# A retention layer and two gated layers on one core: loads, q scaling and the state sum of the first sequence set in another order

## The chip, the cores and the metric

The kernel runs on one core of a Trainium2 chip. The metric is the device time of one execution in microseconds; the median of three runs of the kernel before is 584.75 us (584.52 to 586.34). TensorE (PE) multiplies matrices, with its weight loads as a row of their own (PEld), VectorE (DVE), ScalarE (ACT) and GpSimd (POOL) do the elementwise work, and SyncE (SP) issues all DMAs.

## The reference

Three layers in a row: a linear attention with a decaying state, and two layers of the form "expand to 2048, nonlinearity, contract to 512" on 1536 tokens. The weights come as 64-bit floats.

```
state = gamma * state + k[t] (outer) v[t]      # 2 sequences, 8 heads, 768 steps, head size 64
y[t]  = q[t] @ state / sqrt(64)
h = y @ w_in;  g = max(h, 0) + alpha * min(h, 0);  x = g @ w_out
h = x @ w2_in; g = (a0 + a1 h + a2 h^2 + a3 h^3) / (1 + |b0||h| + |b1| h^2 + 1e-6);  out = g @ w2_out
```

## The kernel before

The attention is done in chunks of 128 steps, six to a sequence, chunks 0 to 5 and 6 to 11. For a chunk c, `att_b(c)` makes the scores: eight matmuls `sc` of k (transposed) and q, which VectorE multiplies by a table of decays (`dm_sb`) into `s`; and it scales q, in place, by a column of constants on ScalarE and by a table (`dq_sb`) on GpSimd for c < 4, else on VectorE. `att_k(c)` scales k (on GpSimd, or on ScalarE for 4 <= c < 8). `att_c(c)` makes the output in a PSUM bank `y`: eight matmuls of v and `s`, then the state product (`st`, eight matmuls of k and v in a bank of their own for the first sequence), then eight matmuls of the state `R` and the scaled q, summed into `y`. The state product is then added to `R` (copied to it for a first chunk), and `y` is split in two rounded parts, `xh` (ScalarE) and `xl` (VectorE, the remainder), so that a product of two such pairs takes three matmuls.

Each of the 64 weight tiles (512 KB as 64-bit words, `r`) is turned into a pair of that kind by `w_abs` (ScalarE), `w_word` in three parts (VectorE: a shift, L284, and two joins, L288 and L292; the tile is `z`), `w_hi` (ScalarE, `wh`) and `w_lo` (VectorE, `wl`). The tables `START` and `dec` (lines 245 to 250 and 482 to 486) say in which half step each of the four is done.

The two gated layers are 96 steps of `pe_h` (twelve matmuls into a bank `h`), a nonlinearity (`act1_*`, `act2_*`) whose result is again split into a pair, and `pe_out` (twelve matmuls into four accumulator banks, `acc`). Chunks 4 to 11 of the attention run between the first steps; `stages` says where. The order of each engine's queue is the order of the code: `tc.manual_schedule()` moves nothing. So an operation that waits holds up whatever stands behind it on its engine.

PSUM has eight banks: a ring of four (`rbank`; scores, `h`, and for chunks from 4 on `y` and `st` too) and the four accumulators (`abank`, which chunks 0 to 3 use for `y` and `st`). SBUF tiles come from a list of 42 slots that are used in turn (`alloc`, `drop`). DMAs all go through SyncE's queue, in code order, eight in flight: the ninth is issued when the first has landed. `keep_warm` puts matmuls of zeros between the first chunks.

The stretch at the start is written out in a list:

```
order = [("b", 0), ("c", 0), ("b", 1), ("b", 2), ("c", 1), ("b", 3), ("c", 2), ("c", 3)]
```

after which the loop over steps begins with h0 (step 0), chunk 4's `att_c`, chunk 5's `att_b`, h1, chunk 5's `att_c`, chunk 6's `att_b`, h2, and `pe_out(0)`.

Of the kernel before, what the change touches and what calls it, by code (L numbers as in the profile page):

```python
# [14 lines left out]
P = 128  # L15
# [3 lines left out]
NK = 4  # L19
# [12 lines left out]
def tile_fused(  # L32
# [71 lines left out]

    def load_nv(c):
        nc.sync.dma_start(out=att[c]["k"], in_=kn[c])
        nc.sync.dma_start(out=att[c]["v"], in_=vn[c])

# [17 lines left out]
    def rows(c, j):  # L126
# [3 lines left out]
        return [(h[1], h[0]), (h[0], h[1])]  # L130

    def att_b(c, bank):
        a = att[c]
        ps = [bank(f"sc{c}_{e}") for e in range(2)]
        for j in range(NK):
            js = slice(j * P, (j + 1) * P)
            for e in range(2):
                es = slice(64 * e, 64 * e + 64)
                nc.tensor.matmul(ps[e][:, js], a["t"][es, js], a["q"][es, js], start=True, stop=True)  # L139
        a["s"] = alloc(f"s{c}")  # L140
        for e in range(2):
            es = slice(512 * e, 512 * e + 512)
            nc.vector.tensor_tensor(out=a["s"][:, es], in0=ps[e], in1=dm_sb[:, es], op=ALU.mult)  # L143
        if c % CPB > 0:
            a["qs"] = a["t"] if c > CPB else a["q"]
            for j in range(NK):
                js = slice(j * P, (j + 1) * P)
                o = 8 * CPB + 4 * (c % CPB) + j
                for ds, es in rows(c, j):
                    nc.scalar.mul(a["qs"][ds, js], a["q"][es, js], cst_sb[es, o:o + 1])  # L150
            eng = nc.gpsimd if c < 4 else nc.vector
            eng.tensor_tensor(out=a["qs"], in0=a["qs"], in1=dq_sb, op=ALU.mult)

    def att_c(c, ybank, pbank):
# [13 lines left out]
        for j, e in heads:  # L168
# [7 lines left out]
            )  # L176
        if not last:
            pst = ys[0][:, 256:512] if four else pbank(f"st{c}")[:, 0:256]
            for j, g in heads:
# [7 lines left out]
                    stop=not four or (first and j == NK - 1),  # L187
                )
        if not first:
            for j, e in heads:  # L190
# [8 lines left out]
                )  # L199
        if not last:  # L200
            src = pst.rearrange("p (j d) -> p j d", j=NK)
            if first:
                nc.scalar.copy(R, src)
            else:
                nc.vector.tensor_tensor(out=R, in0=R, in1=src, op=ALU.add)
        b, o = divmod(c * P, TB)
        osl = slice(o, o + P)
        for n, y in enumerate(ys):
# [6 lines left out]
            )  # L215
        for nm in ("qk", "kv", "s"):
            drop(a[nm])

# [27 lines left out]
    for m in A:  # L246
        START[0, m, 0], START[0, m, 1] = 2 * m - 9, 2 * m - 4
    START[0, 0, 0] = -10
    for j, m in enumerate(B):
# [76 lines left out]
    def pe_h(i):  # L326
        l, b, m, _, _ = STEPS[i]
        wh, wl = W[l, m, 0]
        ps = ring.tile([P, 512], F32, tag="ring", name=f"h{i}")
        n = 0  # L330
        for k in range(NK):
            ks = slice(k * P, (k + 1) * P)
            for w, hl in ((wh, 0), (wh, 1), (wl, 0)):
                nc.tensor.matmul(ps, w[:, ks], xs(hl, b, k, ALL), start=(n == 0), stop=(n == 11))  # L334
                n += 1
        H[i] = ps
# [91 lines left out]
    def act2_split(i):  # L428
        gh, gl = G[i]
        a, t = T3.pop(i)  # L430
        nc.scalar.copy(gh, a)  # L431
        eng = nc.gpsimd if i < NSTEP - 2 else nc.vector
        eng.tensor_tensor(out=gl, in0=a, in1=gh.bitcast(F32), op=ALU.subtract)  # L433
        drop(t)
# [49 lines left out]
    for k, e in enumerate(SEQ):  # L484
        for o, nm in zip((0, 1, 2, 3) if k != 1 else (0, 2, 3, 3), ("abs", "word", "hi", "lo")):
            dec.setdefault(START[e] + o, []).append((nm, k))
# [3 lines left out]
    def half(t, scalar_last=None, between=None):  # L490
# [21 lines left out]
        if later and t % 2 == 0:  # L512
            split_x(*later.pop(0))
        load_next(3 if t < -6 else 4 if t < 2 * N1 else 2)

    with tc.manual_schedule():
# [6 lines left out]
        nc.scalar.preload_act_table_set("natural_log_exp_and_others")  # L523
        for c in range(4):
            att_tiles(c)
# [3 lines left out]
        load_nv(0)  # L529
        load_kq(1)  # L530
        load_next(1)
        load_kq(2)
        load_nv(1)
        nc.sync.dma_start(out=dq_sb, in_=dq)
        load_kq(3)
        load_nv(2)
        load_nv(3)
        load_next(3)
        nc.sync.dma_start(out=alpha_sb, in_=alpha)
        nc.sync.dma_start(out=ab_sb[:, 0:4], in_=pa.partition_broadcast(P))  # L540
# [9 lines left out]
        for n, (s, c) in enumerate(order):  # L550
            if n in (1, 2, 3):
                keep_warm((3, 2, 3)[n - 1])
            if s == "b":
                att_k(c)
                att_b(c, rbank)
            else:
                att_c(c, abank(c % 2), abank(2 + c % 2))
                if c < 2:
                    att_load(4 + c)
            if n == 6:  # L560
                nc.scalar.activation(bb_sb[:, 0:2], ab_sb[:, 4:6], AF.Abs)
                nc.scalar.mul(nalpha_sb, alpha_sb, -1.0)
            half(n - NPRE)
        drop(wt)
        att_b(4, rbank)
# [8 lines left out]
        def stage(t):  # L574
# [12 lines left out]
            else:  # L587
                att_c(c, rbank, rbank)
                if c + 2 < NCH:
# [109 lines left out]
```

## Time and profile before

| | |
|---|---|
| runs, median (range) | 584.75 us (584.52 to 586.34) |
| profiled execution | 586.74 us |
| its span, first to last instruction | 585.0 us |
| mean granted TensorE clock | 0.997 |
| TensorE busy | 574.4 us, 98% of the span |
| VectorE, ScalarE, GpSimd busy | 468.5, 370.8, 75.4 us |
| DMA traffic | 50.78 MB; 341 GB/s on average over the first 60 us |

The profiled execution is one execution, with its own time; the views below are all of it. A timeline row gives the start from the beginning of the span, the duration, engine, line, operation, what it writes and reads, how many were merged, and in brackets how long the engine had been idle and what ended that. TensorE does a float32 matmul in two passes, so eight of them show as x16; a group is as long as the distance to the next group's start, and its last matmul's end is modelled. The granted clock is a share of 2.4 GHz: 0.50 is 1.2 GHz.

### The profile page before, as it was taken

The page shows a single profiled execution, that of the slowest core. Times are in us where ns is not written, and L with a number is a line of the kernel's source. Part 1 is how long each engine was busy: PE and PEld are TensorE (multiplying, and loading weights), DVE is VectorE, ACT ScalarE, POOL GpSimd, SP SyncE. Part 2 cuts the span into 40 slices and gives each one's busy share as a digit, 9 for nine tenths or more (in the row PEclk, how much of TensorE's full clock was granted, in tenths as well). Part 3 has the DMA queues.
Part 4 walks back from the last instruction along what each step waited for, and adds up shares of the span by engine and source line. Part 5 has one row for each costly group of instructions (what it writes and reads, how often), then busy time and mean ns, then how long its engine had stood idle before and what let it go on. Part 6 is the DMA issues. An engine that isn't in the chain of part 4 may idle for free.

```text
span 585.0 us, 8123 instructions
## 1 busy us (share of the span) xinstructions
PE 574.4 (98%) x3040; PEld 473.3 (81%) x3040; DVE 468.5 (80%) x739; ACT 370.8 (63%) x679; POOL 75.4 (13%) x60
## 2 busy tenths in 40 slices
PE   7989999999999999999999999999999999999996
PEld 7868777888888888888888888888888888888885
DVE  1899778778684364448998999999998999887886
ACT  2586667666553353436765787777786786686672
POOL 1402000000000000000000313213222221221220
PEclk8999999999999999999999999999999999999999
DMA  8999422334321012112551010001111100010101
GB/s 315 358 379 347 144 74 73 109 108 145 108 73 36 1 36 73 36 37 72 182 213 37 1 37 29 20 25 37 36 38 36 38 0 1 1 72 2 64 9 73
DMA packets 18920, 50.78 MB, mean 87 GB/s; under 512 B 2624, under 2 KB 2752, under 8 KB 18880
## 3 DMA queue, kind: packets, MB, share of 16 engines
q1 hardware_dynamic: 18880, 50.26, 24.4%
q8 instruction: 24, 0.39, 0.3%
q14 instruction: 16, 0.13, 0.1%
HBM read 47.10 MB, written 3.15 MB: 86 GB/s over the span
## 4 chain that ended last, share of the span: by engine, by line
PE 91%; DVE 5%; ACT 2%; DMA 1%; issue 1%; SPq 0%; ACTq 0%
PE acc L351 43%; PE h L334 43%; PE sc L139 1%; PE y L170 1%; DMA kv<-in_vn_dram 1%; PE y L193 1%; ACT qk L150 1%; DVE z L288 1%; DVE z L292 1%; DVE wl L309 0%; DVE p L448 0%; DVE s L143 0%; PE y L182 0%; ACT kv L120 0%; ACT g L431 0%
## 5 line engine op out<-in xcount | busy, mean ns | idle before, releaser
L334 PE MATMUL h<-xh,wh 128*128 128x512 f32 x384 | 150.3, 391 | 1.5 <-DVE xl L213 1.5
L334 PE MATMUL h<-xl,wh 128*128 128x512 f32 x384 | 149.6, 389 | 0.0
L334 PE MATMUL h<-xh,wl 128*128 128x512 f32 x384 | 149.5, 389 | 0.0
L351 PE MATMUL acc<-wh,g 128*128 128x512 f32 x384 | 126.0, 390 | 0.4 <-ACT g L431 0.4
L433 POOL TENSOR_TENSOR g<-as,g 128x512 fp32r<-128x512 f32 x46 | 62.9, 1367 | 449.5 <-PE acc L351 266.3
L351 PE MATMUL acc<-g,wh 128*128 128x512 f32 x384 | 118.9, 391 | 0.0
L334 PEld LDWEIGHTS h<-xh,wh 128*128 128x128 f32 x384 | 72.1, 188 | 17.1 <-DVE xl L213 1.7
L351 PEld LDWEIGHTS acc<-wh,g 128*128 128x128 f32 x384 | 72.0, 188 | 16.1 <-ACT g L431 0.9
L334 PEld LDWEIGHTS h<-xh,wl 128*128 128x128 f32 x384 | 72.1, 188 | 15.2
L334 PEld LDWEIGHTS h<-xl,wh 128*128 128x128 f32 x384 | 72.1, 188 | 15.0 <-DVE xl L213 0.2
L351 PEld LDWEIGHTS acc<-g,wh 128*128 128x128 f32 x384 | 71.6, 188 | 15.5 <-issue 0.7
L303 ACT CAST wh<-z 128x512 fp32r<-128x512 f32 x64 | 39.6, 619 | 57.2 <-DVE z L292 57.2
L351 PE MATMUL acc<-g,wl 128*128 128x512 f32 x192 | 74.9, 390 | 0.1
L351 PE MATMUL acc<-wl,g 128*128 128x512 f32 x192 | 74.7, 389 | 0.0
L375 DVE SCALAR_TENSOR_TENSOR np<-np,nalpha_sb 128x512 f32<-128x512 f32 x48 | 35.9, 748 | 40.5 <-ACT np L370 40.4
L369 ACT ACTIVATE np<-h 128x512 f32<-128x512 f32 x48 | 28.5, 594 | 44.3 <-PE h L334 44.2
L396 ACT ACTIVATE as<-h 128x512 f32<-128x512 f32 x48 | 28.6, 596 | 41.1 <-PE h L334 41.1
L292 DVE SCALAR_TENSOR_TENSOR z<-r,z 128x512 uint32<-128x512 uint32 x64 | 46.9, 733 | 1.5
L402 DVE SCALAR_TENSOR_TENSOR as<-as,bb_sb,rr 128x512 f32<-128x512 f32 x48 | 36.9, 768 | 13.2 <-ACT rr L397 13.2
L385 DVE TENSOR_TENSOR g<-np,g 128x512 fp32r<-128x512 f32 x48 | 33.1, 689 | 17.6 <-ACT g L380 17.3
L288 DVE SCALAR_TENSOR_TENSOR z<-r,z 128x512 uint32<-128x512 uint32 x64 | 45.6, 712 | 1.0
L309 DVE TENSOR_TENSOR wl<-z,wh 128x512 fp32r<-128x512 f32 x64 | 45.9, 717 | 0.1
(59 smaller groups left out, 751.1 us busy)
## 6 DMA issues: line engine op xcount, KB each, us to landing
r<-in_w1i_dram SPq DMA_DIRECT2D x16, 512.0 KB, 5.8
r<-in_w1o_dram SPq DMA_DIRECT2D x16, 512.0 KB, 4.3
r<-in_w2i_dram SPq DMA_DIRECT2D x16, 512.0 KB, 3.7
r<-in_w2o_dram SPq DMA_DIRECT2D x16, 512.0 KB, 3.3
qk<-in_qT_dram SPq DMA_DIRECT2D x12, 256.0 KB, 6.1
qk<-in_kT_dram SPq DMA_DIRECT2D x12, 256.0 KB, 5.8
kv<-in_kn_dram SPq DMA_DIRECT2D x12, 256.0 KB, 5.7
kv<-in_vn_dram SPq DMA_DIRECT2D x12, 256.0 KB, 5.5
```

What stands on the lines that cost most here:

```text
L288: nc.vector.scalar_tensor_tensor(out=zu, in0=lo, scalar=29, in1=zu, op0=ALU.logical_shift_right, op1=ALU.bitwise_or)
L292: nc.vector.scalar_tensor_tensor(out=zu, in0=hi, scalar=0x80000000, in1=zu, op0=ALU.bitwise_and, op1=ALU.bitwise_or)
L303: nc.scalar.copy(hi, Z[k])
L309: nc.vector.tensor_tensor(out=lo, in0=Z[k], in1=hi.bitcast(F32), op=ALU.subtract)
L334: nc.tensor.matmul(ps, w[:, ks], xs(hl, b, k, ALL), start=(n == 0), stop=(n == 11))
L351: nc.tensor.matmul(acc[0][k], a, c, start=(begin and n == 0), stop=(end != "" and n == 2))
L369: nc.scalar.activation(n, h, AF.Relu, scale=-1.0)
L375: nc.vector.scalar_tensor_tensor(out=p, in0=n, scalar=nalpha_sb[:, m:m + 1], in1=p, op0=ALU.mult, op1=ALU.add)
L385: nc.vector.tensor_tensor(out=gl, in0=p, in1=gh.bitcast(F32), op=ALU.subtract)
L396: nc.scalar.activation(s, h, AF.Square)
L402: nc.vector.scalar_tensor_tensor(out=s, in0=s, scalar=bb_sb[:, 1:2], in1=r, op0=ALU.mult, op1=ALU.add)
L433: eng.tensor_tensor(out=gl, in0=a, in1=gh.bitcast(F32), op=ALU.subtract)
```

## The change

Loads: v of a chunk is loaded before its k; the table `dq` and q and k (transposed) of chunk 2 come ahead of the first weight tile; chunk 4's loads stand among the first, with the third and fourth weight tile between them. The scaling of q is a function of its own, `att_q`: for chunks 1 to 3 it writes a new tile (`qs`), so that it need not wait for the scores, and it is called one chunk ahead. k is scaled later. In `att_c`, the first sequence has the state product behind the product with the state, and the sum of the state behind the split of `y`; the second sequence keeps the old order. Chunks 4 and 5 use accumulator banks for `y` and `st`. The first step's twelve matmuls have those with `xl` last. The second weight tile starts one half step later, with its four parts in four half steps. There are four keep-warm matmuls instead of eight. The last step but one has its split on GpSimd, as all before it.

```diff
     def load_nv(c):
+        nc.sync.dma_start(out=att[c]["v"], in_=vn[c])
         nc.sync.dma_start(out=att[c]["k"], in_=kn[c])
-        nc.sync.dma_start(out=att[c]["v"], in_=vn[c])
...
+    def att_q(c):
+        if c % CPB == 0:
+            return
+        a = att[c]
+        a["qs"] = a["t"] if c > CPB else a["q"]
+        if c < 4:
+            a["qt"] = alloc(f"qs{c}")
+            a["qs"] = a["qt"][:, 0:512]
+        for j in range(NK):
+            js = slice(j * P, (j + 1) * P)
+            o = 8 * CPB + 4 * (c % CPB) + j
+            for ds, es in rows(c, j):
+                nc.scalar.mul(a["qs"][ds, js], a["q"][es, js], cst_sb[es, o:o + 1])
+        eng = nc.gpsimd if c < 4 else nc.vector
+        eng.tensor_tensor(out=a["qs"], in0=a["qs"], in1=dq_sb, op=ALU.mult)
...
-        if c % CPB > 0:
-            a["qs"] = a["t"] if c > CPB else a["q"]
...
+        if c >= 4:
+            att_q(c)
...
-        if not last:
+        def st_part():
             pst = ys[0][:, 256:512] if four else pbank(f"st{c}")[:, 0:256]
...
+            return pst
+
+        if four and not last:
+            pst = st_part()
         if not first:
...
+        if not four and not last:
+            pst = st_part()
+        def state_sum():
+            if not last:
+                src = pst.rearrange("p (j d) -> p j d", j=NK)
+                if first:
+                    nc.scalar.copy(R, src)
+                else:
+                    nc.vector.tensor_tensor(out=R, in0=R, in1=src, op=ALU.add)
+
+        if four:
+            state_sum()
         b, o = divmod(c * P, TB)
...
+        if not four:
+            state_sum()
...
-    START[0, 0, 0] = -10
+    START[0, 0, 0], START[0, 1, 0] = -10, -6
...
+        prs = [(k, w, hl) for k in range(NK) for w, hl in ((wh, 0), (wh, 1), (wl, 0))]
+        if i == 0:
+            prs.sort(key=lambda e: e[2])
...
-        eng = nc.gpsimd if i < NSTEP - 2 else nc.vector
+        eng = nc.gpsimd if i < NSTEP - 1 else nc.vector
...
-        for o, nm in zip((0, 1, 2, 3) if k != 1 else (0, 2, 3, 3), ("abs", "word", "hi", "lo")):
+        for o, nm in zip((0, 1, 2, 3) if k else (0, 0, 2, 2), ("abs", "word", "hi", "lo")):
...
         load_nv(0)
         load_kq(1)
+        nc.sync.dma_start(out=dq_sb, in_=dq)
+        load_kq(2)
         load_next(1)
-        load_kq(2)
         load_nv(1)
-        nc.sync.dma_start(out=dq_sb, in_=dq)
         load_kq(3)
         load_nv(2)
         load_nv(3)
+        load_next(2)
+        load_kq(4)
         load_next(3)
+        load_nv(4)
+        load_next(4)
...
-            if n in (1, 2, 3):
-                keep_warm((3, 2, 3)[n - 1])
+            if n in (1, 3):
+                keep_warm(2)
             if s == "b":
-                att_k(c)
                 att_b(c, rbank)
+                if c < 3:
+                    att_q(c + 1)
+                for k in ((0,), (), (1,), (2, 3))[c]:
+                    att_k(k)
             else:
                 att_c(c, abank(c % 2), abank(2 + c % 2))
...
-                att_c(c, rbank, rbank)
+                if c < CPB:
+                    att_c(c, abank(c % 2), abank(2 + c % 2))
+                else:
+                    att_c(c, rbank, rbank)
```

What this does to the queues shows at three places. The first is GpSimd's queue from its first real operation on; `kv0` to `kv3` are the tiles with k of chunks 0 to 3, `qk1` to `qk3` (before) and `qs1` to `qs3` (after) their q. Before:

```order
L123 TENSOR_TENSOR kv0_96<-kv0_96,cst_sb_67 128x512
L123 TENSOR_TENSOR kv1_98<-kv1_98,cst_sb_67 128x512
L152 TENSOR_TENSOR qk1_97<-qk1_97,dq_sb_73 128x512
L123 TENSOR_TENSOR kv2_100<-kv2_100,cst_sb_67 128x512
L152 TENSOR_TENSOR qk2_99<-qk2_99,dq_sb_73 128x512
L123 TENSOR_TENSOR kv3_102<-kv3_102,cst_sb_67 128x512
L152 TENSOR_TENSOR qk3_101<-qk3_101,dq_sb_73 128x512
```

And after:

```order
L146 TENSOR_TENSOR qs1_153<-qs1_153,dq_sb_73 128x512
L123 TENSOR_TENSOR kv0_96<-kv0_96,cst_sb_67 128x512
L146 TENSOR_TENSOR qs2_197<-qs2_197,dq_sb_73 128x512
L146 TENSOR_TENSOR qs3_224<-qs3_224,dq_sb_73 128x512
L123 TENSOR_TENSOR kv1_98<-kv1_98,cst_sb_67 128x512
L123 TENSOR_TENSOR kv2_100<-kv2_100,cst_sb_67 128x512
L123 TENSOR_TENSOR kv3_102<-kv3_102,cst_sb_67 128x512
```

k of chunk 0 moved behind one q multiply, and k of chunk 1 behind all three. The second place is ScalarE's queue after the change, from chunk 1's q on; `R` is the state, `st0` the first state product, `z0` and `wh0_0` belong to the first weight tile:

```order
L144 ACTIVATE qs1_153<-qk1_97,cst_sb_67 128x128 x4
L232 CAST xh0_75<-y0_0_163 128x4x128
L220 COPY R_72<-st0_172 128x256
L144 ACTIVATE qs2_197<-qk2_99,cst_sb_67 128x128 x4
L301 ACTIVATE z0_203<-r0_116 128x512
L144 ACTIVATE qs3_224<-qk3_101,cst_sb_67 128x128 x4
L232 CAST xh0_75<-y1_0_231 128x4x128
```

The copy of the state stands ahead of the q of chunks 2 and 3. The third is VectorE's queue from the q multiply of chunk 4 to the first join of the fourth weight tile (`r3`); `wl0_1` is the low part of the second tile, which h1 uses, `s5` the scores of chunk 5. Before:

```order
L152 TENSOR_TENSOR qk4_171<-qk4_171,dq_sb_73 128x512
L284 TENSOR_SCALAR z2_350<-z2_350 128x512
L309 TENSOR_TENSOR wl0_1_398<-z0_199,wh0_1_397 128x512
L288 SCALAR_TENSOR_TENSOR z2_350<-r2_126,z2_350 128x512
L292 SCALAR_TENSOR_TENSOR z2_350<-r2_126,z2_350 128x512
L205 TENSOR_TENSOR R_72<-R_72,st4_415 128x256
L213 TENSOR_TENSOR xl1_79<-y4_0_406,xh1_76 128x4x128
L143 TENSOR_TENSOR s5_451<-sc5_0_441,dm_sb_74 128x512
L143 TENSOR_TENSOR s5_451<-sc5_1_442,dm_sb_74 128x512
L152 TENSOR_TENSOR qk5_258<-qk5_258,dq_sb_73 128x512
L284 TENSOR_SCALAR z2_350<-z2_350 128x512
L288 SCALAR_TENSOR_TENSOR z2_350<-r3_227,z2_350 128x512
```

And after:

```order
L146 TENSOR_TENSOR qk4_103<-qk4_103,dq_sb_73 128x512
L307 TENSOR_SCALAR z2_346<-z2_346 128x512
L311 SCALAR_TENSOR_TENSOR z2_346<-r2_130,z2_346 128x512
L315 SCALAR_TENSOR_TENSOR z2_346<-r2_130,z2_346 128x512
L233 TENSOR_TENSOR xl1_79<-y4_0_403,xh1_76 128x4x128
L222 TENSOR_TENSOR R_72<-R_72,st4_420 128x256
L159 TENSOR_TENSOR s5_448<-sc5_0_438,dm_sb_74 128x512
L159 TENSOR_TENSOR s5_448<-sc5_1_439,dm_sb_74 128x512
L146 TENSOR_TENSOR qk5_260<-qk5_260,dq_sb_73 128x512
L307 TENSOR_SCALAR z2_346<-z2_346 128x512
L332 TENSOR_TENSOR wl0_1_396<-z0_203,wh0_1_395 128x512
L311 SCALAR_TENSOR_TENSOR z2_346<-r3_134,z2_346 128x512
```

`wl0_1` moved from ahead of the split of chunk 4 to behind s and q of chunk 5, and the state sum behind the split.

## Rows read from the trace of the kernel before

**Rows 1.** The page, part 1: busy us of each engine, share of the span, instructions.

```profile
PE 574.4 (98%) x3040; PEld 473.3 (81%) x3040; DVE 468.5 (80%) x739; ACT 370.8 (63%) x679; POOL 75.4 (13%) x60
```

**Rows 2.** Waits of TensorE, 0 to 60 us: total us, times, longest.

```profile
PE y L170 <- DMA kv<-in_vn_dram: 2.0, 1, 2.0
PE h L334 <- DVE xl L213: 1.5, 1, 1.5
...
PE y L193 <- DVE R L205: 0.7, 2, 0.5
```

**Rows 3.** Busy us by stretch: stretch, length, PE PEld DVE ACT POOL, granted clock, DMA.

```profile
42.48:577.40 534.92, 534.47 (x2604) 439.88 (x2604) 436.73 (x688) 348.30 (x620) 66.18 (x49) 1.00 0.19 65
```

**Rows 4.** Timeline of GpSimd, 8 to 24 us: start, us, engine, line, operation, idle before.

```profile
8.49 1.04 POOL L123 TENSOR_TENSOR kv<-kv,cst_sb 128x512 f32<-128x512 f32 x1 [8.05 <-DMA kv<-in_kn_dram]
...
15.12 1.27 POOL L152 TENSOR_TENSOR qk<-qk,dq_sb 128x512 f32<-128x512 f32 x1 [0.38 <-ACT z L278]
...
18.35 1.72 POOL L152 TENSOR_TENSOR qk<-qk,dq_sb 128x512 f32<-128x512 f32 x1
20.03 1.49 POOL L123 TENSOR_TENSOR kv<-kv,cst_sb 128x512 f32<-128x512 f32 x1
```

**Rows 5.** Timeline of SyncE's DMA issues, 9.5 to 15 us.

```profile
9.67 0.33 SPq L102 DMA_DIRECT2D qk<-in_qT_dram  x1
10.35 0.33 SPq L103 DMA_DIRECT2D qk<-in_kT_dram  x1
11.62 0.33 SPq L106 DMA_DIRECT2D kv<-in_kn_dram  x1
```

**Rows 6.** Timeline of ScalarE, 11 to 23 us.

```profile
11.98 0.37 ACT L203 COPY R<-st 128x256 f32<-128x256 f32 x1 [9.97 <-PE st L182]
...
14.44 0.66 ACT L278 ACTIVATE z<-r 128x512 f32<-128x512 f32 x1
15.21 1.28 ACT L150 ACTIVATE qk<-qk,cst_sb 128x128 f32<-128x128 f32 x4
```

**Rows 7.** Timeline of TensorE, 8 to 36 us.

```profile
10.85 1.09 PE L182 MATMUL st<-kv 128*64 128x64 f32 x16
...
16.69 0.64 PE L182 MATMUL st<-kv 128*64 128x64 f32 x16
17.25 1.09 PE L193 MATMUL y<-qk,R 64*64 64x128 f32 x16
18.27 1.16 PE L139 MATMUL sc<-qk 64*128 64x128 f32 x16
19.36 1.09 PE L170 MATMUL y<-s,kv 128*64 128x128 f32 x16
20.29 0.63 PE L182 MATMUL st<-kv 128*64 128x64 f32 x16
...
34.81 0.50 PE L334 MATMUL h<-xh,wh 128*128 128x512 f32 x1
...
35.39 0.39 PE L334 MATMUL h<-xh,wl 128*128 128x512 f32 x1
```

**Rows 8.** Timeline of VectorE, 16 to 42 us.

```profile
18.97 1.65 DVE L292 SCALAR_TENSOR_TENSOR z<-r,z 128x512 uint32<-128x512 uint32 x1
...
36.54 0.42 DVE L284 TENSOR_SCALAR z<-z 128x512 uint32<-128x512 uint32 x1
...
39.33 0.68 DVE L309 TENSOR_TENSOR wl<-z,wh 128x512 fp32r<-128x512 f32 x1
```

**Rows 9.** Busy us by stretch, around the low clock (columns as in rows 3).

```profile
9.12:12.30 3.18, 3.18 (x34) 3.06 (x35) 0.00 (x0) 0.32 (x2) 0.41 (x1) 0.50 1.03 388
```

**Rows 10.** Timeline of VectorE, 571 to 578 us.

```profile
572.69 0.69 DVE L433 TENSOR_TENSOR g<-as,g 128x512 fp32r<-128x512 f32 x1
```

**Rows 11.** Timeline of TensorE, 576.3 to 579 us.

```profile
577.46 0.50 PE L351 MATMUL acc<-wh,g 128*128 128x512 f32 x1 [0.43 <-ACT g L431]
```

**Rows 12.** The page, part 5: out<-in, count, busy us, mean ns, idle before.

```profile
L433 POOL TENSOR_TENSOR g<-as,g 128x512 fp32r<-128x512 f32 x46 | 62.9, 1367 | 449.5 <-PE acc L351 266.3
```

More of the change, by code (lines that the diff above doesn't have):

```diff
@@ L143, in att_b @@
             nc.vector.tensor_tensor(out=a["s"][:, es], in0=ps[e], in1=dm_sb[:, es], op=ALU.mult)
-        if c % CPB > 0:
-            a["qs"] = a["t"] if c > CPB else a["q"]
[L146 to L152, printed above, removed]
+        if c >= 4:
+            att_q(c)
     def att_c(c, ybank, pbank):
@@ L199, in att_c @@
                 )
[L200 to L205, printed above, removed]
+        if not four and not last:
[9 more added lines that the diff above has]
+            state_sum()
         b, o = divmod(c * P, TB)
@@ L215, in att_c @@
             )
-        for nm in ("qk", "kv", "s"):
-            drop(a[nm])
+        if not four:
+            state_sum()
+        for nm in ("qk", "kv", "s", "qt"):
+            if nm in a:
+                drop(a[nm])
     raw = {}
@@ L329, in pe_h @@
         ps = ring.tile([P, 512], F32, tag="ring", name=f"h{i}")
-        n = 0
-        for k in range(NK):
+        prs = [(k, w, hl) for k in range(NK) for w, hl in ((wh, 0), (wh, 1), (wl, 0))]
+        if i == 0:
+            prs.sort(key=lambda e: e[2])
+        for n, (k, w, hl) in enumerate(prs):
             ks = slice(k * P, (k + 1) * P)
-            for w, hl in ((wh, 0), (wh, 1), (wl, 0)):
-                nc.tensor.matmul(ps, w[:, ks], xs(hl, b, k, ALL), start=(n == 0), stop=(n == 11))
-                n += 1
+            nc.tensor.matmul(ps, w[:, ks], xs(hl, b, k, ALL), start=(n == 0), stop=(n == 11))
         H[i] = ps
@@ L513, in half @@
             split_x(*later.pop(0))
-        load_next(3 if t < -6 else 4 if t < 2 * N1 else 2)
+        load_next(3 if t < -8 else 4 if t < 2 * N1 else 2)
     with tc.manual_schedule():
@@ L523, in tile_fused @@
         nc.scalar.preload_act_table_set("natural_log_exp_and_others")
-        for c in range(4):
+        for c in range(5):
             att_tiles(c)
@@ L550, in tile_fused @@
         for n, (s, c) in enumerate(order):
-            if n in (1, 2, 3):
-                keep_warm((3, 2, 3)[n - 1])
+            if n in (1, 3):
+                keep_warm(2)
             if s == "b":
-                att_k(c)
                 att_b(c, rbank)
+                if c < 3:
+                    att_q(c + 1)
+                for k in ((0,), (), (1,), (2, 3))[c]:
+                    att_k(k)
             else:
                 att_c(c, abank(c % 2), abank(2 + c % 2))
[L558 to L562, printed above, removed]
+                if c == 1:
+                    att_load(5)
             half(n - NPRE)
+        nc.scalar.activation(bb_sb[:, 0:2], ab_sb[:, 4:6], AF.Abs)
+        nc.scalar.mul(nalpha_sb, alpha_sb, -1.0)
         drop(wt)
```

## The prediction

> **What bounds the kernel now.** I read the busy table first. The reader is to see that TensorE is busy for 574.4 of 585.0 us [rows 1], so a change that leaves its matmuls alone can only touch the remaining 10.6 us, stretches at half clock, and gaps that a new wait would open. Next the waits of TensorE: those of more than half a microsecond all lie before 43 us [rows 2], and from 42.48 to 577.40 it is busy for 534.47 of 534.92 us [rows 3]. So a shift of the matmul at 42.48 is carried to the end one for one, and only what comes before it and the last step count. Then the timelines of the other engines up to 42 us, for what releases TensorE there, and the granted clock, which was 0.50 for the 3.18 us from 9.12 [rows 9], after TensorE had waited 2.0 us for v of chunk 0 [rows 2].
>
> The profiled execution took 586.74 us, 1.74 of it outside the span; the runs' median is 584.75, 2.0 lower. I work out a difference on the profiled execution and add it to both: the prediction is on the median's scale. 0.3% of it is 1.75 us, about what a measurement of this kernel can tell from no change.
>
> **The first chunk and GpSimd's queue.** v of chunk 0 now comes before its k. A transfer in that place had landed when GpSimd started at 8.49 [rows 4], so the first product may start at 8.5 instead of 9.12. That gains nothing, because of what is next. On GpSimd the multiply of chunk 1's q by dq now stands ahead of the scaling of chunk 0's k, and the state product of chunk 0 needs that k. The q multiply waits for dq, the ninth transfer. Eight are in flight, so the issue of transfer n+8 shows when transfer n has landed: the seventh by 9.67, the eighth by 10.35, and the ninth, then a weight tile twice as large, by 11.62 [rows 5]. At 0.68 us for a transfer of dq's size it lands at 11.0. Multiply 1.27 [rows 4], then k 1.04 [rows 4]: k is ready at 13.3, where it was ready at 9.53. So the state product, at 10.85 before [rows 7], starts at 13.4. The two keep-warm groups that shrank or went lie in this gap, so they give nothing.
>
> **From the first state to the state product of chunk 1.** In ScalarE's order the copy of the state is ahead of the scaling of chunk 2's q, then come a weight's absolute value and chunk 3's q. GpSimd does the q of chunks 2 and 3 before k of chunk 1. The chain: state product 0.64 at full clock, 1.09 at half [rows 7], to 14.0 or 14.5; copy 0.37, q2 1.28, absolute value 0.66, q3 1.28 [rows 6], 3.6 in all, to 17.6 or 18.1 (its two inputs come in time: at 0.68 for each 256 KB behind dq the weight tile lands near 13.7 and q3 near 15.8). GpSimd: q3 1.27 to 1.72, k 1.04 to 1.49 [rows 4], to 19.9 or 21.3. So the state product of chunk 1 starts at 19.95 to 21.3. What TensorE has to do in between, even at half clock, ends before that, so the wait is for GpSimd.
>
> The longer durations in that range are those that GpSimd had at 18.35 and 20.03, beside VectorE's operation that took 1.65 [rows 8], against 0.68 for one of its kind with GpSimd idle, at 39.33 [rows 8]. The Trainium skill, "SBUF — State Buffer", section "SBUF: two separate sides", says that GpSimd and a VectorE operation with two SBUF inputs hold one port pair in turn, each for its whole instruction. The trace agrees with it, and here it speaks against the change: the weight's three operations on VectorE now meet two q multiplies and a k in a row. By that rule the late end of the range holds, without it the early one.
>
> **From there to the second step's matmul (h1).** Before, 16.69 to 34.81 us is 18.12 us. Its groups by their starts [rows 7]: state product 0.56, product with the state 1.02, scores 1.09, product with v 0.93. After the change the same stretch has four state products, three of each of the others and twelve matmuls of h0 at 0.23, 14.1 us; the product with the state of chunk 1 now stands ahead of it. So before had 18.12 - 1.02 - 14.1 = 3.0 us of waits and gaps in it. The waits for the state sum go (0.7 [rows 2], with the gaps around them), since the products with the state now follow the sum at a distance, and so does that of the scores for a bank that the sum gives back, since chunks 4 and 5 now use the accumulators' banks. Two come in their place: the state sum now follows the split of y on VectorE, so chunk 3's product with the state waits for cast, split and sum, about 0.3 longer than the state product and the next product with v; and s of chunk 4 stands behind a whole weight chain, about 0.4. With 0.5 for gaps, 15.3 us. So h1 starts at 35.25 to 36.6, against 34.81: **+0.45 to +1.8**. Against the nearest rows (half clock at the start, GpSimd's long operations) I take **+1.1**.
>
> **h1 waits for a weight.** The second weight tile's START moved by one half step, and its low part now stands behind s of chunk 5, its q multiply and a shift on VectorE. h1's third matmul needs that low part, and s of chunk 5 needs the scores just ahead of h1. In rows of before: the shift starts at 36.54 and takes 0.42, a low part takes 0.68 [rows 8], so it is there at about 37.6, where the third matmul started at 35.39 [rows 7]. That is a new wait of 2.2 us; behind it queue the products of chunk 5, its scores' successors and h2. What goes is the wait of h2, 1.5 us [rows 2]: its bank was chunk 5's, given back by the split; now that lies in an accumulator's bank, and the accumulator's first matmul comes some 3 us after the split, so no wait takes its place. Net **+0.7**. It could be as low as -1.5, if something kept the scores late enough for the low part to come first, and no higher than +2.2. The rest of VectorE's queue moves by 0.6 for the added operation, less than TensorE does. h0 with its xl matmuls last has its cover in the 0.5 of gaps.
>
> **The last step.** Its predecessor's split goes to GpSimd and leaves VectorE's queue, where it took 0.69 us [rows 10], less with the overlap to its neighbours. The last matmuls, which waited 0.43 for the last cast at 577.46 [rows 11] and then for the last split, come that much earlier: **-0.55**, between 0 and -0.8. GpSimd takes 1.37 for it [rows 12], to about 574.1; TensorE, which does twelve such matmuls in 2.7 us and is done with this step at 577, needs it near 574.7. Were GpSimd held up past that, the gain would go.
>
> **Sum.** +1.1 + 0.7 - 0.55 = +1.25: 588.0 us on the profiled execution's scale, **586.0** on the median's. Its own range runs from 584.9 (+0.45, +0.3, -0.6) to 586.9 (+1.8, +0.7, -0.4).
>
> **Rivals.** (1) *The clock falls again in h1's wait.* It fell after the 2.0 us without work and did not after the 1.5 of h2 [rows 2]; 2.2 is just over the larger. It would then run at 0.50 for about 3.2 us, of which half is lost: +1.6, 587.6 us, clearly slower. For it: the length. Against: the stretch around it is denser than at 7 us. The Trainium skill, "TensorE: Matmul & The Clock Gate", section "HAM oscillation — how this bites in real kernels", describes just such a loss after every long wait; the trace shows one fall, at 9 us, and cannot show this one. This rival decides as soon as the wait is 2 us or more. (2) *The removed waits are worth more than the new ones.* The state product of chunk 1 at its earliest (q3 landed 15.8, then 1.28, 1.27 and 1.04: 19.4) and nothing but work behind it, 14.1, put h1 at 33.5, -1.3; with h1's wait covered, -1.5, and -0.55 that is -3.35: 581.4 us, faster; with half of it, 583.1. For it: every wait that the change aims at is in the profile. Against: s of chunk 5 can't run before its scores, and h1 stands right behind these. (3) *The reorder is absorbed*: h1's wait is covered because h1 comes later still, so that +1.1 and +0.7 overlap: +0.3, 585.0, no change.
>
> **Chances.** The forecast 0.45, rival 1 0.30, rival 2 0.12, rival 3 0.13. A fifth of the forecast lies above +1.75, since the late ends of its terms can meet. Faster by over 0.3%: 0.11, rival 2 but for its mildest form; slower by over 0.3%: 0.30 + 0.09 and a little more for a clock that stays low beyond 19 us, 0.41; within: 0.48. The range leaves out the far ends of rival 2 and of rival 1 on top of the late start: 583.2 to 588.4.
>
> **What would show it.** In the changed profile: GpSimd's first operation a q multiply at about 11.0 and k of chunk 0 ending near 13.3; the first state product near 13.4 with TensorE idle ahead of it; the state product of chunk 1 at 20 to 21.3, released by GpSimd; h1's third matmul about 2.2 us behind its second, released by VectorE; no wait of h2; granted clock 0.50 past 13 us, and for rival 1 again near 38; the last cast about 0.55 us earlier against the end of its predecessor's matmuls. A state product of chunk 1 before 18, or a third matmul of h1 without a wait, would make the prediction wrong.

## The result, and the profile after

| | before | after |
|---|---|---|
| median of the runs shown | 584.56 us (six: 583.96 to 586.34) | 589.44 us (six: 587.47 to 590.67) |
| profiled execution | 586.74 us | 589.76 us |
| span; mean granted clock | 585.0 us; 0.997 | 588.0 us; 0.992 |

The ratio is 1.0078, with a 95% interval of 1.0062 to 1.0093: the change makes the kernel slower by 0.8%. The forecast was 586.0 us with a range up to 588.4, so the time lies 1.0 us above the range.

The busy table of the profile after stands beside [rows 1]: VectorE has 2.0 us less, TensorE 0.6 more with eight matmul passes fewer (four matmuls on the zero tile, two passes each).

```profile
PE 575.0 (98%) x3032; PEld 472.9 (80%) x3032; DVE 466.5 (79%) x738; ACT 370.9 (63%) x679; POOL 77.1 (13%) x61
```

The waits of TensorE up to 70 us (after that it has none of note), which answer to [rows 2]:

```profile
PE st L192 <- POOL kv L123: 3.9, 2, 3.4
PE h L358 <- DVE wl L332: 2.2, 1, 2.2
PE warm L545 <- DVE bb_sb L569: 1.1, 1, 1.1
PE y L179 <- DVE s L159: 0.8, 1, 0.8
```

The waits for v of chunk 0, for the state and for h2's bank are gone. GpSimd and the second weight's low part `wl` have taken their place. GpSimd's timeline shows why it is late (before: [rows 4]):

```profile
10.51 1.26 POOL L146 TENSOR_TENSOR qs<-qs,dq_sb 128x512 f32<-128x512 f32 x1 [10.07 <-ACT qs L144]
11.73 1.04 POOL L123 TENSOR_TENSOR kv<-kv,cst_sb 128x512 f32<-128x512 f32 x1
15.62 1.28 POOL L146 TENSOR_TENSOR qs<-qs,dq_sb 128x512 f32<-128x512 f32 x1 [2.85 <-ACT qs L144]
17.34 1.40 POOL L146 TENSOR_TENSOR qs<-qs,dq_sb 128x512 f32<-128x512 f32 x1 [0.44 <-ACT qs L144]
18.70 3.93 POOL L123 TENSOR_TENSOR kv<-kv,cst_sb 128x512 f32<-128x512 f32 x3
```

And TensorE's timeline (before: [rows 7]): the first state product, that of chunk 1, h1 with its third matmul, later matmuls of h1, and h2.

```profile
12.82 1.12 PE L192 MATMUL st<-kv 128*64 128x64 f32 x16 [3.41 <-POOL kv L123]
...
20.24 0.69 PE L192 MATMUL st<-kv 128*64 128x64 f32 x16 [0.50 <-POOL kv L123]
...
35.48 0.50 PE L358 MATMUL h<-xh,wh 128*128 128x512 f32 x1
35.82 0.40 PE L358 MATMUL h<-xl,wh 128*128 128x512 f32 x1
38.46 0.50 PE L358 MATMUL h<-xh,wl 128*128 128x512 f32 x1 [2.25 <-DVE wl L332]
...
40.06 0.63 PE L358 MATMUL h<-xh,wl 128*128 128x512 f32 x1
...
45.67 0.50 PE L358 MATMUL h<-xh,wh 128*128 128x512 f32 x1
```

A matmul of h1 takes 0.39 us before [rows 7] and 0.63 from 40 us on here. The busy times by stretch (columns as in [rows 3]) say why: the granted clock is at its lower level in two stretches, each behind one of the long waits. Before, there is one [rows 9].

```profile
12.82:15.53 2.71, 2.71 (x30) 2.59 (x32) 0.00 (x0) 1.54 (x6) 0.00 (x0) 0.50 1.05 398
39.90:43.20 3.30, 3.30 (x17) 2.35 (x18) 3.25 (x6) 1.12 (x2) 0.00 (x0) 0.50 1.06 358
45.67:580.60 534.93, 534.85 (x2608) 440.19 (x2606) 436.66 (x689) 350.05 (x627) 68.03 (x50) 1.00 0.18 63
```

From 45.67 on TensorE is busy throughout, so the loss stands at h2, 45.67 against 42.48, 3.2 us. From h2 to the last matmul 0.54 us are won; the way out after it took 0.35 more (5.00 us to the span's end against 4.65). In the other profiles below it took 4.5 to 4.6 us in kernels made from the one before and 4.8 to 5.4 in kernels made from the one after, so the change costs a little there too; by what, no run shows. So the profiled executions differ by 3.0 us, the medians by 4.9: this gap is the first thing the experiments had to explain.

### The profile page after: what moved, and what is told of

It reads as the page before. It is cut to its first block, busy times and chain, and to the rows that moved or that the text cites. A ratio compares the mean times of both kernels' runs of the same rounds, so it can differ in the third digit from the quotient of the medians.

```text
span 588.0 us, 8106 instructions
## 1 busy us (share of the span) xinstructions
PE 575.0 (98%) x3032; PEld 472.9 (80%) x3032; DVE 466.5 (79%) x738; ACT 370.9 (63%) x679; POOL 77.1 (13%) x61
## 4 chain that ended last, share of the span: by engine, by line
PE 94%; ACT 1%; DVE 1%; DMA 1%; POOL 1%; SPq 1%; issue 0%; POOLq 0%
PE acc L374 44%; PE h L358 44%; PE y L179 2%; PE sc L155 2%; PE y L207 1%; DMA dq_sb<-in_dq_dram 1%; PE st L192 1%; ACT qk L144 1%; DVE p L471 0%; POOL qs L146 0%; POOL kv L123 0%; ACT qs L144 0%; PE y L192 0%; DVE qk L146 0%; DVE wl L332 0%; ACT z L301 0%
## 5 line engine op out<-in xcount | busy, mean ns | idle before, releaser
L456 POOL TENSOR_TENSOR g<-as,g 128x512 fp32r<-128x512 f32 x47 | 64.6, 1375 | 452.3 <-PE acc L374 266.7
L315 DVE SCALAR_TENSOR_TENSOR z<-r,z 128x512 uint32<-128x512 uint32 x64 | 45.6, 713 | 1.5
L311 DVE SCALAR_TENSOR_TENSOR z<-r,z 128x512 uint32<-128x512 uint32 x64 | 45.0, 704 | 1.0
```

The costliest lines, as they stand in the source:

```text
L311: nc.vector.scalar_tensor_tensor(out=zu, in0=lo, scalar=29, in1=zu, op0=ALU.logical_shift_right, op1=ALU.bitwise_or)
L315: nc.vector.scalar_tensor_tensor(out=zu, in0=hi, scalar=0x80000000, in1=zu, op0=ALU.bitwise_and, op1=ALU.bitwise_or)
```

## The experiments

Kernels of the same runs share the kernel before (median 584.4 to 584.5 us in each). Each median is of 6 to 12 executions.

**The kernel before, again.** No edit.

> The kernel before, unchanged, once more. It asks what the granted clock is in its usual executions: its profiled execution took 586.74 us, 2.2 us over its median, with a mean clock of 0.997 and one stretch at 0.50 from 9.1 to 12.3 us. Theory: the usual execution is without that stretch, so the mean clock is 0.999 to 1.000 at about 584.5 us, and the comparison by medians (after +4.9 us) is made against a start at full clock, the comparison by profiles (+3.0 us) against a start with one loss. Rival: the usual execution has the low stretch as well and the profile is merely longer; then its clock reads 0.997 at 584.5 us. Both expect a ratio of 1.000.

Measured: 584.73 us, ratio 1.0008 (0.9997 to 1.002). Its profiled execution took 584.43 us at a clock of 1.000. Busy times by stretch, the start and from h2 to the last matmul:

```profile
7.70:12.30 4.60, 3.46 (x55) 3.17 (x55) 1.75 (x4) 1.64 (x5) 1.04 (x1) 1.00 1.04 401
...
40.16:578.00 537.84, 537.33 (x2615) 441.96 (x2616) 437.99 (x692) 348.37 (x620) 66.57 (x49) 1.00 0.19 67
```

There is no low stretch at the start, and TensorE waited 1.1 us for v of chunk 0 there, not 2.0 [rows 2]; h1 comes at 32.49 and h2 at 40.16, not 34.81 and 42.48. Of 117 executions of this kernel in all sets of runs here, 7 had a clock of 0.997 or less, with a median of 586.7; the others had 584.4. The profile that the prediction read is of the kind of the 7. Against the usual execution the change loses 3.0 us up to h1 (35.48 - 32.49) and 2.5 more up to h2 (10.19 us from h1 to h2 against 7.67).

**After, with the second weight tile made as before.**

```
-    START[0, 0, 0], START[0, 1, 0] = -10, -6
+    START[0, 0, 0] = -10
...
-        for o, nm in zip((0, 1, 2, 3) if k else (0, 0, 2, 2), ("abs", "word", "hi", "lo")):
+        for o, nm in zip(((0, 0, 2, 2), (0, 2, 3, 3))[k] if k < 2 else (0, 1, 2, 3), ("abs", "word", "hi", "lo")):
```

> The kernel after, with the second weight tile made as before (its low part ahead of the state, no wait for it at h1). Theory: the wait of 2.25 us at h1 goes, the 1.5 us wait at h2 comes back in part, and with the long wait the second low stretch of the clock (39.9 to 43.2 us, about 1.7 us lost) goes too: h2 at 42 to 43 instead of 45.67, and about 3 us less than after, 586 us (585.3 to 587). Rival A (the clock falls at that place whatever the wait is, or its fall costs nothing): only the net wait of 0.7 us is gained, 588.7 us. Rival B (the loss of the change is all in the late start of st and y): no gain, 589.4 us.

Measured: 586.32 us. h1 has no wait and is followed by h2 in 6.09 us (36.12 to 42.21), at full clock. The theory's number held, both rivals miss by 2.4 us or more; but the part of h2's wait that it expected back did not come. What is left is the wait for GpSimd's k, in two places (TensorE's waits), and in this execution the clock fell behind the second of them, of 1.71 us (busy times by stretch, from that state product on):

```profile
PE st L192 <- POOL kv L123: 4.5, 2, 2.8
```

```profile
19.34:24.00 4.66, 4.66 (x56) 4.04 (x58) 3.69 (x6) 0.68 (x1) 1.94 (x2) 0.65 1.05 369
```

**After, with k ahead of q on GpSimd.**

```
+                att_k(c)
                 att_b(c, rbank)
                 if c < 3:
                     att_q(c + 1)
-                for k in ((0,), (), (1,), (2, 3))[c]:
-                    att_k(k)
```

> The kernel after, with GpSimd scaling k ahead of q in each chunk, as before, the rest of the change left in. st0 can start at about 11 instead of 12.82, and st1, which is released by GpSimd's k of chunk 1, at about 16.5 instead of 20.24. Theory: h1 comes to 32 to 33.5 instead of 35.48, but the low part of the second weight tile is on VectorE behind the same loads, so that the wait at h1 gets no shorter and the clock falls there again: 0 to 3 us less than after, 587.5 us. Rival B (the loss is the late start alone): 584.5 us or less, and no low stretch at h1. Rival C (the order on GpSimd is worth nothing, VectorE and ScalarE bound the start): 589.4 us.

Measured: 586.58 us. The state products start at 8.55 and 14.76, h1 at 30.60, 4.9 us earlier. Much of that is waited off at h1, whose wait grew (TensorE's waits), and the clock fell in it (busy times by stretch):

```profile
PE h L358 <- DVE wl L332: 3.1, 1, 3.1
```

```profile
7.00:30.60 23.60, 22.11 (x322) 18.46 (x321) 16.59 (x29) 13.75 (x39) 9.08 (x7) 1.00 1.02 371
33.40:40.00 6.60, 5.59 (x20) 4.17 (x22) 5.65 (x11) 2.18 (x4) 0.00 (x0) 0.50 1.05 386
```

Up to h1 the clock is at 1.00, with the same four keep-warm matmuls, so the fall at the start goes with GpSimd's order and not with the four that were taken out. ScalarE stood 2.51 us for the small load pb in this run, which the later kernels take up. The theory's range holds, at its far end; the start alone is not the loss.

**After, with work in h1's wait.**

```
             nc.tensor.matmul(ps, w[:, ks], xs(hl, b, k, ALL), start=(n == 0), stop=(n == 11))
+            if i == 1 and n == 1:
+                keep_warm(7)
```

The zero tile and `keep_warm` are defined earlier for it, and the tile's slot is given back after h1 instead of ahead of chunk 4.

> The kernel after, with seven matmuls on a tile of zeros put into TensorE's queue just ahead of the first matmul of h1 that waits for the low part of the second weight tile. The wait itself stays; TensorE works in it. They write an accumulator bank that nothing reads. Theory: without the gap the clock stays at 1.00 from 39.9 to 43.2 us, h2 comes 1.5 to 1.8 us earlier, and the time is about 1.7 us less than after, 587.7 us. Rival: the fall of the clock there isn't caused by the gap, or costs nothing that isn't made up later; then 589.4 us, or a little more.

Measured: 588.44 us in six executions, 0.8 under the kernel after (589.27 over its twelve), less than the 1.7 expected and within the spread. In its profile the wait has shrunk to 0.68 us, the clock is 1.00 from 35.4 to 43.5, and h2 follows h1 in 8.59 us, against 10.19. Four of its executions still had a clock of 0.993, so it fell more than once elsewhere; where, no profile shows. By itself this run is inconclusive.

**The kernel after, again.** No edit.

> The kernel after, unchanged, once more, for more executions of it beside those of its parts. Theory: 589.2 us (588.7 to 589.7); its executions fall apart by the mean granted clock, those at 0.997 some 2 us below those at 0.991 to 0.992, by whether the clock fell once or twice. Rival: the time does not go with the clock.

Measured: 589.26 us. Over the twelve executions of both sets, five have a clock of 0.997 and a median of 587.6, seven have 0.991 to 0.994 and 589.7. The profiled one is of the first kind. It has the same wait at h1 (TensorE's timeline), and no fall behind it; h2 follows h1 in 8.62 us. In the busy times by stretch the clock falls at the start, and is up in the wait and from there to h2:

```profile
37.51 0.51 PE L358 MATMUL h<-xh,wl 128*128 128x512 f32 x1 [2.25 <-DVE wl L332]
```

```profile
11.89:15.30 3.41, 3.41 (x34) 3.07 (x34) 0.27 (x1) 2.27 (x7) 0.65 (x1) 0.51 1.05 386
34.52:37.51 2.99, 0.74 (x5) 0.30 (x3) 2.93 (x7) 2.99 (x8) 0.00 (x0) 1.00 1.04 414
37.51:43.14 5.63, 5.63 (x58) 4.47 (x58) 5.00 (x9) 2.58 (x7) 0.00 (x0) 1.00 1.04 357
```

So a wait of 2.25 us leads to a fall in some executions and not in others. Where it does, it costs 10.19 - 8.62 = 1.6 us.

**Before, with the low part late alone.**

```
-    START[0, 0, 0] = -10
+    START[0, 0, 0], START[0, 1, 0] = -10, -6
...
-        for o, nm in zip((0, 1, 2, 3) if k != 1 else (0, 2, 3, 3), ("abs", "word", "hi", "lo")):
+        for o, nm in zip((0, 1, 2, 3) if k else (0, 0, 2, 2), ("abs", "word", "hi", "lo")):
```

The last line also puts the first weight tile's four parts into two half steps, as the change does, so the low part is not quite alone; h0, which needs that tile, comes no later in its profile (24.15 us) than in the kernel before (24.93 in its usual execution).

> The kernel before with one other edit of the change alone: the second weight tile's parts put off, its low part behind s of chunk 5. Theory: a wait of about 2.2 us at h1's third matmul, and h2's wait of 1.5 us stays, since chunk 5's bank is given back as much later as h1 is; at 2.2 us the clock falls as in the kernel after, for 1.7 us more: 584.4 + 2.2 + 1.7 = 588.3 us (587.5 to 589). Rival A: the wait alone, the clock stays up: 586.6 us. Rival B: h1's wait is taken out of h2's: 585.1 us.

Measured: 586.58 us (584.41 to 589.92), ratio 1.0026 (1.0007 to 1.0046); the theory's 588.3 is too high. The median equals rival A's 586.6 by luck: A keeps the clock up, and the executions near that time have it down. The profiled execution shows rival B: in TensorE's timeline h1 waits, h2 hardly any more (0.32 instead of 1.52), and in the busy times by stretch the clock stays up.

```profile
34.12 0.50 PE L334 MATMUL h<-xh,wl 128*128 128x512 f32 x1 [2.07 <-DVE wl L309]
...
40.14 0.50 PE L334 MATMUL h<-xh,wh 128*128 128x512 f32 x1 [0.32 <-DVE xl L213]
```

```profile
32.05:34.12 2.07, 0.00 (x1) 0.00 (x0) 2.07 (x5) 2.07 (x5) 0.00 (x0) 1.00 1.01 391
34.12:40.14 6.02, 5.70 (x58) 4.47 (x59) 5.39 (x10) 3.12 (x8) 0.00 (x0) 1.00 1.04 399
```

Three executions are of this kind (clock 1.000, median 584.9, 0.5 over the kernel before). Nine have a clock of 0.994 to 0.997; the seven at 0.996 or 0.997 took 586.2 to 588.3. The edit costs little by its wait and about 2 us by the clock, as far as the mean clock tells it: no profile of the nine was kept.

**The same, with work in the wait.** Eight matmuls of zeros ahead of h1's third one, as above.

> The kernel before with the second weight tile's parts put off, as in the run that came out at 586.58 us, and eight matmuls on a tile of zeros in the wait at h1's third matmul. Of that run's executions three had a mean clock of 1.000 and took 584.4 to 585.1 us, seven had 0.996 or 0.997 and took 586.2 to 588.3. Theory: these two groups are executions in which the clock did not fall and did fall in the wait of 2.07 us; with the wait filled all are of the first kind, 585.0 us, clock 0.998 or more. Rival: the low clock lies elsewhere, at the start, or isn't caused by the gap: two groups as before, median 586.5 us.

Measured: 585.11 us (584.51 to 585.41) in eleven executions, all at 0.998 or more: the theory's number, and the second group is gone. h1's wait is 0.28 us (TensorE's timeline):

```profile
34.70 0.53 PE L345 MATMUL h<-xh,wl 128*128 128x512 f32 x1 [0.28 <-DVE wl L312]
```

That matmul comes 2.81 us behind h1's first, as in the run without the work (2.80), so the work delayed nothing. Apart from the zero tile's slot, which is kept longer, nothing but the gap differs, so the fall of the clock behind h1's wait is caused by the gap: 1.5 us between the medians.

**After, with both edits undone.** The low part and GpSimd's order as before.

> The kernel after with both edits of the two runs before together: the second weight tile made as in the kernel before, and GpSimd scaling k ahead of q. Each of them alone took about 3 us off (586.32 and 586.58 against 589.44). Theory: one was the long wait at h1 with its fall of the clock, the other the late start with its fall of the clock; they are two losses, so the gains add up: 589.4 - 3.1 - 2.9 = 583.4 us (582.5 to 584.0), no wait over 1 us at h1 or h2 and the clock at 1.00 throughout, and so somewhat faster than the kernel before (584.4). Rival: both edits win the same time (what is gained at the start is waited off at h1, or at a later weight), then 586 us.

Measured: 584.47 us (584.11 to 585.61), clock 0.998 or more: 4.8 us under the kernel after, where the two edits alone gave 2.95 and 2.7, and the theory expected 6.0. It is level with the kernel before, not faster. h2 comes at 38.41, 1.75 us ahead of the usual execution before, but the first output matmul that needs a low part then waits. The timelines of TensorE, VectorE and ScalarE, one after the other, lead from its wait back to the load of pb:

```profile
22.77 1.09 PE L207 MATMUL y<-qs,R 64*64 64x128 f32 x16 [1.51 <-DVE R L222]
...
43.50 0.50 PE L374 MATMUL acc<-g,wl 128*128 128x512 f32 x1 [1.53 <-DVE wl L332]
```

```profile
30.77 0.69 DVE L332 TENSOR_TENSOR wl<-z,wh 128x512 fp32r<-128x512 f32 x1 [1.31 <-ACT wh L326]
```

```profile
26.26 0.20 ACT L590 ACTIVATE bb_sb<-ab_sb 128x2 f32<-128x2 f32 x1 [1.21 <-DMA ab_sb<-in_pb_dram]
```

That last operation and the next, which read the small parameters, were also moved by the change, from behind chunk 2's `att_c` to behind chunk 3's; the diff above leaves this out.

**Before, with the banks alone**: `att_c(c, abank(c % 2), abank(2 + c % 2))` for chunks 4 and 5.

> The kernel before with one edit of the change alone: chunks 4 and 5 take their y and st from the accumulators' banks. Theory: the 1.5 us that h2 waited for the split of chunk 5 go, and nothing takes their place, since the accumulator's first matmul comes some 3 us after that split: 584.4 - 1.5 = 582.9 us (582.5 to 583.5). Rival: the wait moves to the accumulator's first matmul or to the scores behind it: 584.4 us.

Measured: 583.36 us, ratio 0.9973 (0.996 to 0.9987). h2 has no wait and follows h1 in 6.08 us instead of 7.67; the accumulator waits 0.59 us for a low part, so the rival holds in part. 1.1 of the 1.5 us is kept.

**Before, with the banks and the last step.** As well `i < NSTEP - 1` in the choice of the engine for the split.

> The kernel before with two edits of the change: chunks 4 and 5 in the accumulators' banks, and the split of the last step but one on GpSimd. The last step ended 0.54 us sooner against h2 in the kernel after. Theory: the two add up, 584.4 - 1.5 - 0.55 = 582.35 us, faster than the kernel before by 0.35%. Rival: the bank is worth nothing: 583.85 us.

Measured: 582.43 us (581.4 to 582.93), ratio 0.9953 (0.9934 to 0.9971), as the theory's sum; its parts by medians are 1.1 and 0.9, not 1.5 and 0.55. It is the best of all kernels run, 2.0 us under the kernel before and 6.8 under the kernel after. Its waits of TensorE:

```profile
PE warm L522 <- DVE bb_sb L542: 1.1, 1, 1.1
PE acc L351 <- DVE wl L309: 0.6, 1, 0.6
PE y L170 <- DMA kv<-in_vn_dram: 0.2, 1, 0.2
PE y L193 <- POOL qk L152: 0.2, 1, 0.2
```

So what is left of the change (loads, q ahead of time, state product and state sum, h0's order, four keep-warm matmuls for eight, the parameters' place) costs 584.47 - 582.43 = 2.0 us. The last four kernels ask where.

**Both edits undone, and the state sum ahead of the split.** `state_sum()` is called in one place, ahead of the split.

> The kernel after with both edits undone as in the run that came out at 584.47 us, and the state sum ahead of the split of y again. There TensorE waited 1.51 us for the state sum in chunk 3. Theory: that wait shrinks by the cast and the split that no longer stand ahead of it, to 0.5 us or less, VectorE's chain from there to the low part that the accumulator's first matmul waits for (1.53 us) starts as much earlier, and the time is 0.6 to 1.1 us less, 583.6 us. Rival: VectorE and ScalarE set the time of that low part whatever the sum does, and what is won at chunk 3 is waited off there: 584.5 us.

Measured: 584.76 us. The wait in chunk 3 is gone, h0 is 1.9 us earlier (23.61), and the first output matmul that needs a low part is where it was (TensorE's timeline):

```profile
43.54 0.50 PE L371 MATMUL acc<-g,wl 128*128 128x512 f32 x1 [1.51 <-DVE wl L329]
```

The rival held.

**The state product ahead of the product with the state as well.** `st_part()` is called in the old place for both sequences.

> As the run with the state sum ahead of the split, and the state product ahead of the product with the state as well, as in the kernel before. What is left of the change are the order of the loads, the q scaled in a tile of its own and ahead of time, the banks, h0's order, the last step. Theory: the state comes about 1 us sooner, no wait for it is left, and the time is that of the kernel before with the banks and the last step alone, 582.4 to 583 us. Rival: the rest of the change (loads and q) costs by itself what the kernel lost, then 584.5 us.

Measured: 584.89 us, again the rival; 43.92 for the same output matmul, behind 1.52. ScalarE stood 1.42 us for pb.

**The parameter loads early**, in two kernels: with both edits undone, and with the state's old order besides.

```
         load_nv(3)
+        nc.sync.dma_start(out=alpha_sb, in_=alpha)
+        nc.sync.dma_start(out=ab_sb[:, 0:4], in_=pa.partition_broadcast(P))
+        nc.sync.dma_start(out=ab_sb[:, 4:6], in_=pb.partition_broadcast(P))
         load_next(2)
...
         load_next(4)
-        nc.sync.dma_start(out=alpha_sb, in_=alpha)
-        nc.sync.dma_start(out=ab_sb[:, 0:4], in_=pa.partition_broadcast(P))
-        nc.sync.dma_start(out=ab_sb[:, 4:6], in_=pb.partition_broadcast(P))
```

> As the run with both edits undone (584.47 us), with the three small parameter loads (alpha, pa, pb) issued ahead of the second weight tile and chunk 4's loads, where the change had put them behind. In that run ScalarE stood 1.21 us for pb at 26.26, VectorE then 1.31 us for the high part of the second weight tile (30.77), and TensorE 1.53 us for the low part of the first output weight (43.50). Theory: these three waits are one chain; with pb early ScalarE starts its q of chunk 4 at 25.1 instead of 26.5, VectorE's wait shrinks to 0.1 or 0.2, and the time is 1.1 to 1.3 us less, 583.3 us. Rival: VectorE is bound by its own work from chunk 3 on, or another load is late then; 584.5 us.

> The same edit on the run with the state product and the state sum in the old order (584.89 us). There ScalarE stood 1.42 us for pb and VectorE 1.83 us for the high part of the second weight tile. Theory: 1.3 to 1.5 us less, 583.5 us, so that the place of the parameter loads is most of what the order of the loads costs against the kernel before with banks and last step alone (582.43 us). Rival: the cost lies in the other loads: 584.9 us.

Measured: 583.79 us, ratio 0.999 (0.9981 to 0.9999), and 583.63 us, ratio 0.9986 (0.9977 to 0.9995): 0.7 and 1.3 us less than without the edit. In the first, ScalarE no longer waits for pb, VectorE not for the high part, and that output matmul is 1.0 us earlier (TensorE's timeline):

```profile
42.51 0.50 PE L374 MATMUL acc<-g,wl 128*128 128x512 f32 x1 [0.40 <-DVE wl L332]
```

The chain from pb to that matmul is shown. It is a third of the 2.0 us in the first kernel and half of 2.5 (584.89 - 582.43) in the second; the theory put it at nearly all. The other 1.2 to 1.4 us stay open. The start is a poor suspect: h0 comes at 25.14 in the second kernel against 24.00 with the banks and the last step alone, but that profile took 581.56 us, 0.9 under its own median, with a wait of 0.2 us for v. The profile with the banks alone (583.42, at its median) has h0 at 25.34, no earlier. Against it the second kernel is 0.3 us late at the output matmul with the low part (TensorE's timelines, banks alone first):

```profile
25.34 0.50 PE L334 MATMUL h<-xh,wh 128*128 128x512 f32 x1
...
42.12 0.50 PE L351 MATMUL acc<-g,wl 128*128 128x512 f32 x1 [0.59 <-DVE wl L309]
```

```profile
42.44 0.50 PE L369 MATMUL acc<-g,wl 128*128 128x512 f32 x1 [0.77 <-DVE wl L327]
```

More is lost behind it: from the first matmul of step 3 to the last matmul it takes 530.82 us (46.42 to 577.24) against 530.29 with the banks and the last step (44.91 to 575.20), where scores wait 0.2 us for a split at 61.86 as they do not in the other, and the way out takes 0.2 more. Which edit does that is not shown.

## Why the prediction was wrong

By medians the change costs 589.27 - 584.49 = 4.8 us, made up so: banks and last step -2.0; the late low part +2.1 (586.58 - 584.47) and GpSimd's order +1.85 (586.32 - 584.47), each as it costs without the other; +0.8 more for both together; loads and the rest +2.0. On the two profiles it is +0.67 up to h1, +2.52 from h1 to h2 (10.19 against 7.67), -0.54 to the last matmul and +0.35 on the way out, 3.0 in all.

*GpSimd's queue: right.* First q multiply forecast at 11.0, k of chunk 0 done at 13.3, state products at 13.4 and 19.95 to 21.3; measured 10.51, 12.77, 12.82 and 20.24, released by GpSimd (the first q multiply itself by ScalarE's part of q, not by dq). One multiply took 1.40 us, not 1.28, while VectorE's timeline has joins of 1.64 and 1.42 instead of 0.69:

```profile
17.65 1.64 DVE L311 SCALAR_TENSOR_TENSOR z<-r,z 128x512 uint32<-128x512 uint32 x1
19.32 1.42 DVE L315 SCALAR_TENSOR_TENSOR z<-r,z 128x512 uint32<-128x512 uint32 x1
```

The Trainium skill, "SBUF — State Buffer", section "SBUF: two separate sides", has whichever of such a pair starts first hold the shared ports for its whole instruction while the other waits. The trace agrees in the main: most of the cost falls on VectorE's joins, and TensorE shows no wait for those.

*From the first chunk to h1: right on the profiled execution, wrong on the median.* This is the step that failed: "I work out a difference on the profiled execution and add it to both". +0.45 to +1.8 was forecast and +0.67 measured, profile against profile. But in the profile before, the clock had fallen at the start, behind a wait for v that was longer than in the usual profile (2.0 us against 1.1), and the mean clock is as low in 7 of 117 executions of that kernel; in all twelve of after it is at 0.997 or less. Against the usual execution the term is 34.52 - 32.49 = +2.0 to 35.48 - 32.49 = +3.0. The sum of +1.25 silently took half clock at the start for the usual start of the kernel before.

*h1's wait: right.* 2.2 us forecast, 2.25 measured, none at h2. Its net of +0.7 is near the +0.95 of the profile without a fall (8.62 against 7.67), but for another reason: the low part alone shrinks h2's wait from 1.5 to 0.3, so the banks had little left to win in the change.

*The clock in h1's wait: the second step that failed.* The likeliest case let it stay up; rival 1 (0.30) had it fall, at +1.6. It cost 1.6 us, and fell in the profiled execution; by the mean clock about seven of the twelve executions of after have a second fall. "Decides as soon as the wait is 2 us or more" is too sharp: at 2.07 and 2.25 us there are executions with and without a fall. The Trainium skill, "TensorE: Matmul & The Clock Gate", section "Part 1: The HAM clock gate (the "warmup" mystery)", says of a kernel's start that the number of matmuls at the lower clock varies between runs of one kernel. Something alike shows here in the middle of one: two executions of the kernel after have the same wait of 2.25 us and clocks of 0.50 and 1.00 behind it.

*Last step: right.* -0.55 forecast; from h2 to the last matmul 537.33 us (45.67 to 583.00) against 537.87 before, -0.54. The cost of [rows 12] stayed hidden. The +0.35 on the way out is a term that the prediction did not have.

*The loads: missed.* The prediction worked out the transfers it saw moved, but not the three small ones that were moved behind by others; in the kernel after, ScalarE does not wait for them, and they bind once GpSimd's order is undone.

With the two steps put right, after the fact and roughly, 584.4 + 1.25 + 2.3 (what the low clock is worth in the kernel before, 586.7 - 584.4) + 7/12 of 1.6 = 588.9, near the 589.3 measured.

## What to carry to other kernels

Before a difference is added to a median, ask whether the profiled execution is a usual one: a profile 2 us over its own median, with a stretch at half clock, is not, and a change that makes that stretch the rule loses what the profile already seems to pay. On an engine that is full from some point on, price a new wait ahead of it twice, once as time and once as clock, and fill it with idle work if it can't be removed. And of a bundle of edits, time the small ones alone: here two small ones won 2.0 us, and the rest cost 6.8.

## What the runs showed of the hardware that was not expected

Whether the clock falls behind a gap is not set by the gap's length alone. It did not fall behind 1.5 us at h2 in any profile. At the start it fell behind the 2.0 us for v in the profile that the prediction read, and not behind 1.8 us in the kernel with the low part late and work in the wait. In the kernel after with the weight put back it fell behind 1.71 us and, in the same execution, not behind 2.76. At 2.07 us three of twelve executions are without a fall, by their clock of 1.000; at 2.25 us one profile has it and one does not. Around 3.1 us it stayed low for 6.6 us, 1.0 of them still in the wait, against 3.3 us in the kernel after. And a load of 1 KB, moved behind five larger ones, held up TensorE 17 us after it landed, by way of ScalarE and VectorE.
